# Infini-attention with a gated routed FFN on one core: moving a ReLU and a copy between engines, merging maxima, and timing small products by their reader

## The chip, the cores and the metric

The kernel runs on one core of one Trainium2 chip. A core has five engines that run their own queues in order and meet through semaphores: TensorE (PE in the profile; its weight loads are PEld), VectorE (DVE), ScalarE (ACT), GpSimd (POOL) and SyncE (SP), which here only issues transfers. The time is the device time of the one launch in microseconds; lower is better. A profile shows one execution.

## The reference

The input `A_x` has 2048 tokens of 640 channels. Two branches are mixed token by token, `g * a + (1 - g) * b`, with `g = sigmoid(x . gate_w)`.

Branch `a` is attention with a compressed memory: 32 heads of 20 channels, four segments of 512 tokens.

```python
for s in range(N):                      # N = 4 segments, one after the other
    qs, ks, vs = q[:, :, s], k[:, :, s], v[:, :, s]
    logits = einsum("bhqd,bhkd->bhqk", qs, ks) * scale + mask      # causal, inside the segment
    a_dot = einsum("bhqk,bhkd->bhqd", softmax(logits), vs)
    pq = phi(qs)                        # phi(t) = t + 1 where t > 0, exp(t) elsewhere
    a_mem = einsum("bhld,bhde->bhle", pq, M) / (einsum("bhld,bhd->bhl", pq, z)[..., None] + 1e-6)
    outs.append(g * a_mem + (1.0 - g) * a_dot)                     # g = sigmoid(beta), per head
    pk = phi(ks)
    M = M + einsum("bhld,bhle->bhde", pk, vs);  z = z + einsum("bhld->bhd", pk)
a = concat(outs) @ wo
```

Branch `b` picks the one token with the largest `x . w_r`, runs a SwiGLU FFN with 1728 hidden channels on it alone, and adds the result, weighted by a sigmoid, to that token; all other tokens pass through.

## The kernel before

**Units, jobs, groups.** The 32 heads are two halves of 16. A unit is one half and one segment, so there are eight units, `u` = 0 to 7, the four segments of the first half and then those of the second. A unit has five projection jobs (`projections`, L658): two for q and k over 512 columns, one over 256, two for v over 320 or 322. A job is 15 steps in each of two phases (`pair_up`, L373): every step issues two 64-row matmuls at L392 that run side by side into two PSUM banks. All numbers are split into a high and a low part, and three products (high·high, high·low, low·high) make one product in near full precision. Between the phases stands a drain (the "swap"), because each bank then gets the other half of the rows.

**Projected tiles.** `evac_t` (L460) brings a tile of q or k to SBUF as `phi` (L474 on ScalarE for the even bank, L477 on VectorE for the odd one) and queues "pieces". One splits it into hi (ScalarE, L486) and lo (GpSimd, L490); these go to DRAM and come back stacked as `qs` and `ks`, four places each. Two other pieces make phi(t) = max(t, 0) + exp(min(t, 0)): `neg` = ReLU(−t) on ScalarE (L501), `neg` = exp(−neg) on ScalarE (L507), ReLU of the tile in place on ScalarE (L509), and the sum on GpSimd (L511). `neg` has a single buffer. There are five `phi` places; a projection job waits when they would run out.

**Attention.** A group `n` is four heads of a unit: 32 groups. A group goes through five `a` steps (`a_step`, L724), which compute logits with the query on the partition and take their maximum on VectorE: blocks of 128 queries by up to 512 keys, causal ones through added matmuls with `tri` and `eye`. Steps 0 and 1 hold one block of 512 keys, steps 2 and 3 a block of 384 beside one of 128, step 4 four blocks of 256 at once. L749 issues one reduction per block, L745 one for all of step 4. The maxima are split (GpSimd, L763 and L764), transposed (`m_rows`, L767) and sent into two more rows of `qs`. Then five `b` steps (`b_step`, L789) compute the logits again, with the key on the partition and the maximum subtracted inside the matmul; ScalarE takes the exponential into one of eight `p` places (L800), and GpSimd zeroes what is not causal (L806). `pv_step` (L814) multiplies with v in 32 matmuls of 128×32 shape and ScalarE copies the result to `pvs` (L827), which has one place. `norm` (L841) transposes it, divides by the sum on VectorE (L860 to L865) and adds the memory part on GpSimd (L868).

**Memory.** `keys` (L552) transposes phi(k), `memory_write` (L592) adds to M and z, `memory_read` (L566) computes the memory part of a group. The reads, the writes and PV use the 128×32 shape of the array; projections, logits and transposes use 64×128.

**Output.** When all projections are issued, 16 output tiles follow (`out_stage`, L1092), each after its rows came back from DRAM and were transposed (`out_rows`, L1049: hi on ScalarE at L1066, lo on VectorE at L1068). The FFN runs as a side job between them and the attention.

**What sets the order.** The program is written out by a planner at build time (the loop at L1245). It keeps a modelled time for every engine (`now`), adds an estimate for each operation (`run`, `pe`), and always issues what its model says is ready: transposes of maxima and `turned` work first (transposes of keys, normalisation), then PV, then logits, then one projection step. Four PSUM banks serve projections and small products: two take the sums of the current job, and the other two (`misc`) take PV, reads, writes and transposes. At the next job the pairs swap, so a small product must be read before that.

```python
def misc_ready(n=1, keep=KEEP):                                     # L352
    if filling[0] and not full() and (where[0] == "open" or where[0] == "mid" and left[0] < keep):
        return 1e9
```

`left` is the modelled time still to go in the job, `KEEP` is 1.2 us (1.6 for output tiles). Logits are held back to 2.9 groups behind the projections' progress (`chunks`):

```python
if e and e[1] <= t and e[0] + LEAD <= chunks[0] + ahead and (best is None or e[0] < best[1][0]):   # L1212
```

Memory reads and writes are `chores`; `visit` (L1226) issues those that fit its budget, then PV.

Of the kernel before, what the change touches and what calls it, by code (L numbers as in the profile page):

```python
# [46 lines left out]
LEAD = 2.9  # L47
PR = 8
# [4 lines left out]
KEEP = 1.2  # L53
OKEEP = 1.6
# [11 lines left out]
def tile_infini_mod(  # L66
# [285 lines left out]
    def misc_ready(n=1, keep=KEEP):  # L352

        if filling[0] and not full() and (where[0] == "open" or where[0] == "mid" and left[0] < keep):
            return 1e9
        return sorted(misc_free[i] for i in others())[n - 1]
# [16 lines left out]
    def pair_up(o0, f0, o1, f1, cols, note):  # L373


        n = 3 * KT
        left[0] = 2 * n * us_of(cols)
        for phase in range(2):
            if phase:
                where[0] = "swap"  # L380
                yield 0.0
                nc.tensor.drain()
                pe(0.12)
            use((64, 128))
            where[0] = "mid"
            for i in range(n):
                step_at[0] = max(f(i, r)[2] for f, r in ((f0, phase), (f1, 1 - phase)))
                while step_at[0] > now["PE"]:
                    yield 0.0
                for o, f, r in ((o0, f0, phase), (o1, f1, 1 - phase)):  # L390
                    a, b, ready = f(i, r)
                    nc.tensor.matmul(o, a, b, start=phase == 0 and i == 0, stop=phase == 1 and i == n - 1)  # L392
                note(phase, i)
                left[0] -= us_of(cols)
                yield pe(us_of(cols)) - 0.22
# [60 lines left out]
    phis = {}  # L456

    uses = {}

    def evac_t(u, j, sums, parts):  # L460
# [34 lines left out]
        if s < SEG - 1 or j in QGROUP:  # L495
            state = {}
            uses[u, j] += 1 + (s < SEG - 1) + (s > 0 and j in QGROUP)

            def part():
                r = state["r"] = pool.tile([128, L], F32, tag="neg", bufs=1, name="neg")  # L500
                nc.scalar.activation(r, c, AF.Relu, scale=-1.0)  # L501
                run("ACT", 0.2 + L / 1200, free)

            def rest():
                used()
                r = state["r"]
                nc.scalar.activation(r, r, AF.Exp, scale=-1.0)  # L507
                run("ACT", 0.2 + L / 1200)
                nc.scalar.activation(c, c, AF.Relu)  # L509
                end = run("ACT", 0.2 + L / 1200, split_at[0])  # L510
                nc.gpsimd.tensor_tensor(out=c, in0=c, in1=r, op=OP.add)  # L511
                end = run("POOL", 0.1 + L / 430, end)
                if s < SEG - 1:
                    turned.append((end, lambda: (used(), keys(u, j, c)), lambda: writes[0] == epoch(u)))
# [3 lines left out]
            pieces.extend(((1, part, False), (1, rest, False)))  # L518

# [25 lines left out]
    def first(entries, t, budget=1e9):  # L545

        for e in entries:
            if e[0] <= t and e[-1]() and (len(e) == 3 or e[1] <= budget):
                entries.remove(e)
                return e  # L550

    def keys(u, j, e):  # L552
        keyed[u] = keyed.get(u, 0) + 1
        for r in range(2):
            parts = [t for t in TILES[j] if t[2] == "k" and t[0] // 64 == r]
            if parts:
# [5 lines left out]
                end = pe(0.25)  # L562
                for r0, r1, kind, g, c0 in parts:
                    nc.scalar.copy(kk[:, g, :, c0:c0 + r1 - r0], tp[:, :, r0 - 64 * r:r1 - 64 * r])
                    misc_free[i] = run("ACT", 0.3, end)

    def memory_read(u, g, e):
# [6 lines left out]
        end = pe(0.75, mbd_at[0])  # L574
# [6 lines left out]
        misc_free[i] = run("ACT", 0.55, mid)  # L581
# [9 lines left out]
    def memory_write(u):  # L591
# [9 lines left out]
        end = pe(2.6, va_at[0])  # L601
# [28 lines left out]
    def turn():  # L630
        e = first(turned, now["PE"]) if misc_ready(2) <= now["PE"] else None
        if e:
            e[1]()
            return True
# [89 lines left out]
    def a_step(n, k):  # L724
        use((64, 128))
        if n not in mx:
            mx[n] = pool.tile([128, 2, 2, 4], F32, tag="mx", bufs=3, name="mx")
# [16 lines left out]
        if k == 4:  # L744
            nc.vector.tensor_reduce(out=mx[n][:, :, :, 1], in_=a.rearrange("p b (c t) -> p b c t", c=2), axis=AX.X, op=OP.max)  # L745
            end = run("DVE", 0.16 + 2 / 0.96 * 0.512, end)
        else:
            for i, p, at, w in LOGITS[k]:
                nc.vector.tensor_reduce(out=mx[n][:, :, p, i:i + 1], in_=a[:, :, at:at + w], axis=AX.X, op=OP.max)  # L749
# [9 lines left out]
    def m_split(n):  # L759
        m = mx.pop(n).rearrange("p b c i -> p b (c i)")  # L760
# [6 lines left out]
    def m_rows():  # L767
        if not rows or rows[0][0] > now["PE"] or misc_ready(2) > now["PE"]:
            return False
# [3 lines left out]
        for r in range(2):  # L773
# [5 lines left out]
            misc_free[i] = run("ACT", 0.2, end)  # L779
# [9 lines left out]
    def b_step(n, k):  # L789
# [11 lines left out]
        end = run("ACT", 1.05, end)  # L801
# [12 lines left out]
    def pv_step(n):  # L814
# [12 lines left out]
        nc.scalar.copy(pvs[n], pv)  # L827
        misc_free[i] = run("ACT", 0.6, end)
        turned.append((misc_free[i] + 0.1, lambda: norm(n), lambda: True))
# [11 lines left out]
    def norm(n):  # L841
# [16 lines left out]
        end = pe(0.47)  # L858
# [190 lines left out]
    def out_rows(t):  # L1049
# [12 lines left out]
        done = pe(0.6, ot_at[t])  # L1062
# [21 lines left out]
    def ahead(t):  # L1084
# [3 lines left out]
        if t in ot and not tasks and not loaded and ot_at[t] <= now["PE"] and misc_ready(2, OKEEP) <= now["PE"] + 0.4:  # L1088
            out_rows(t)
            return True  # L1090

    def out_stage():  # L1092
# [3 lines left out]
        for t in range(NT):  # L1096
# [35 lines left out]
            end = misc_free[pair[0]] = run("DVE", 0.5, now["PE"] + 0.22, mixed[t])  # L1132
            half = pool.tile([128, L], F32, tag="neg", bufs=1, name="half")[:, :n]
# [74 lines left out]
    def logits(ahead, t):  # L1208
# [13 lines left out]
    def pv_ready(t):  # L1222
        n = done_pv[0]
        return n < NG and done_b[0] > n and n - 1 not in pvs and p_at[n] <= t and misc_ready() <= t

    def visit(budget, pv):  # L1226
# [6 lines left out]
        for f in side:  # L1233
            if f.last == 2 and side_at[0] <= now["PE"] and misc_ready() <= now["PE"] + 0.2:
                f.step()
# [9 lines left out]
    while True:  # L1245
# [15 lines left out]
        if pv and (where[0] == "open" or blocked or gt > 1e8 or left[0] > 2.0 or over[0] == JOBS * NU):  # L1261
            logits(0.2, t)
            visit(0.7 if where[0] == "mid" else 1.3, True)
            continue
        waits = t - side_at[0] if side and side[0].last == 2 else -1.0
        if where[0] == "swap" and (old or waits >= 0.0) and misc_ready() <= t + 0.2:
            logits(0.2, t)
# [3 lines left out]
        if waits > 3.0 and misc_ready() <= t:  # L1271
            visit(0.7, False)
            continue
        if logits(0.0, t):
# [4 lines left out]
        if logits(1.0 if gt < 1e8 else 99.0, t):  # L1279
# [59 lines left out]
```

## Time and profile before

| | |
|---|---|
| median of 3 runs | 607.3 us (604.44 to 608.02) |
| the profiled execution | 608.08 us, its span 606.4 us |
| TensorE busy | 572.0 us, 94% |
| ScalarE | 383.9 us, 63% |
| VectorE | 338.1 us, 56% |
| GpSimd | 327.0 us, 54% |
| granted TensorE clock | 0.993 |

The span runs from the first to the last instruction of the one profiled execution. Busy time is the union of an engine's instructions, so a busy TensorE can still be slower than it might be. In lists of groups, the number after `x` counts instructions, then come busy us and the mean ns of one, and behind the bar the idle time of that engine just before them with what ended it. A wait "A <- B" is idle time of A's engine that an instruction of B ended; where several things were waited for it names the last.

### The profile page before, as it was taken

The page shows a single profiled execution, that of the slowest core. Times are in us where ns is not written, and L with a number is a line of the kernel's source. Part 1 is how long each engine was busy: PE and PEld are TensorE (multiplying, and loading weights), DVE is VectorE, ACT ScalarE, POOL GpSimd, SP SyncE. Part 2 cuts the span into 40 slices and gives each one's busy share as a digit, 9 for nine tenths or more (in the row PEclk, how much of TensorE's full clock was granted, in tenths as well). Part 3 has the DMA queues.
Part 4 walks back from the last instruction along what each step waited for, and adds up shares of the span by engine and source line. Part 5 has one row for each costly group of instructions (what it writes and reads, how often), then busy time and mean ns, then how long its engine had stood idle before and what let it go on. Part 6 is the DMA issues. An engine that isn't in the chain of part 4 may idle for free.

```text
span 606.4 us, 19959 instructions
## 1 busy us (share of the span) xinstructions
PE 572.0 (94%) x8186; PEld 456.3 (75%) x8186; DVE 338.1 (56%) x614; ACT 383.9 (63%) x681; POOL 327.0 (54%) x443
## 2 busy tenths in 40 slices
PE   6998999999989999999999899999999879989896
PEld 5886976877767877676887667787677667778896
DVE  7433555664565546854556466665465496643432
ACT  8726775876677667766755667675575565555332
POOL 4554656556556966758635634864685343333111
PEclk9999999999989999999999989999999999999999
DMA  7886757536845677678798887576686793424561
GB/s 196 224 277 203 223 149 229 140 126 188 210 135 132 184 211 188 189 213 238 233 274 218 253 245 236 142 239 189 211 239 198 209 262 104 144 82 139 164 197 66
DMA packets 81331, 116.73 MB, mean 193 GB/s; under 512 B 36112, under 2 KB 41752, under 8 KB 81240
## 3 DMA queue, kind: packets, MB, share of 16 engines
q1 hardware_dynamic: 81240, 115.46, 65.1%
q8 instruction: 65, 1.06, 0.8%
q14 instruction: 26, 0.21, 0.1%
HBM read 72.94 MB, written 41.96 MB: 189 GB/s over the span
## 4 chain that ended last, share of the span: by engine, by line
PE 79%; DMA 8%; DVE 5%; ACT 3%; issue 2%; POOL 2%; SPq 1%; POOLq 0%; ACTq 0%; DVEq 0%
PE bank L392 45%; PE bank L821 10%; PE bt L796 7%; PE a L732 6%; DVE mx L749 2%; PE bank L573 2%; PE bank L600 2%; DMA stkk<-hi 2%; PE a L741 2%; DMA raw<-in_xT_dram 2%; SPq L153 1%; PE bank L857 1%; ACT p L800 1%; PE bank L965 1%; DMA ot<-otok 1%
## 5 line engine op out<-in xcount | busy, mean ns | idle before, releaser
L749 DVE TENSOR_REDUCE mx<-a 128x2 f32<-128x768 f32 (+1 forms) x192 | 160.7, 865 | 96.3 <-PE a L741 47.3
L800 ACT ACTIVATE p<-bt 128x1024 f32<-128x1024 f32 x160 | 164.2, 1026 | 60.8 <-PE bt L796 56.3
L806 POOL TENSOR_SCALAR_AFFINE_SELECT p<-p 128x512 f32<-128x512 f32 (+1 forms) x160 | 88.0, 550 | 129.4 <-ACT p L800 103.4
L392 PE MATMUL bank<-xhi,whi 64*128 64x512 f32 (+1 forms) x480 | 101.7, 380 | 2.9 <-issue 0.5
L392 PE MATMUL bank<-xlo,whi 64*128 64x512 f32 (+1 forms) x480 | 101.1, 373 | 0.6 <-POOL xlo L181 0.6
L392 PE MATMUL bank<-xhi,wlo 64*128 64x512 f32 (+1 forms) x480 | 99.4, 368 | 0.0
L732 PE MATMUL a<-ks,qs 60*128 60x384 f32 (+3 forms) x512 | 74.4, 326 | 7.9 <-DVE mx L749 6.3
L796 PE MATMUL bt<-qs,ks 62*128 62x128 f32 (+3 forms) x512 | 75.5, 333 | 4.4 <-ACT p L800 3.7
L821 PE MATMUL bank<-p,va 128*32 128x512 f32 (+3 forms) x1024 | 75.5, 435 | 0.0
L392 PEld LDWEIGHTS bank<-xhi,whi 64*128 64x128 f32 x480 | 56.1, 187 | 14.5 <-issue 11.5
L796 PEld LDWEIGHTS bt<-qs,ks 62*128 62x128 f32 x512 | 49.2, 188 | 18.6 <-issue 7.6
L821 PEld LDWEIGHTS bank<-p,va 128*32 128x32 f32 x1024 | 30.1, 109 | 42.4 <-issue 30.2
L732 PEld LDWEIGHTS a<-ks,qs 60*128 60x128 f32 x512 | 50.2, 187 | 14.6 <-DVE mx L749 8.2
L511 POOL TENSOR_TENSOR phi<-phi,neg 128x512 f32<-128x512 f32 x38 | 49.0, 1288 | 22.4 <-ACT phi L509 20.0
L392 PEld LDWEIGHTS bank<-xlo,whi 64*128 64x128 f32 x480 | 57.5, 188 | 4.0 <-POOL xlo L181 1.6
L490 POOL TENSOR_TENSOR lo<-phi,hi 128x512 fp32r<-128x512 f32 x40 | 51.9, 1298 | 14.7 <-ACT hi L486 7.0
L392 PE MATMUL bank<-whi,xhi 64*128 64x322 f32 (+1 forms) x320 | 58.2, 325 | 1.5
L392 PEld LDWEIGHTS bank<-xhi,wlo 64*128 64x128 f32 x480 | 57.0, 187 | 2.5
L392 PE MATMUL bank<-whi,xlo 64*128 64x322 f32 (+1 forms) x320 | 57.5, 318 | 0.0
L392 PE MATMUL bank<-whi,oh 64*128 64x320 f32 x320 | 51.8, 322 | 6.0 <-DVE ol L1068 4.0
L392 PE MATMUL bank<-wlo,xhi 64*128 64x322 f32 (+1 forms) x320 | 57.3, 319 | 0.0
L827 ACT COPY pvs<-bank 128x512 f32<-128x512 f32 x32 | 18.8, 587 | 56.5 <-PE bank L821 56.4
(119 smaller groups left out, 1088.9 us busy)
## 6 DMA issues: line engine op xcount, KB each, us to landing
qs<-stkq SPq DMA_DIRECT2D x64, 240.0 KB
ks<-stkk SPq DMA_DIRECT2D x64, 240.0 KB
raw<-in_xT_dram SPq DMA_DIRECT2D x40, 256.0 KB
stkq<-hi SPq DMA_DIRECT2D x32, 320.0 KB
stkq<-lo SPq DMA_DIRECT2D x32, 160.0 KB
otok<-ou SPq DMA_DIRECT2D x32, 160.0 KB
xf<-in_x_dram SPq DMA_DIRECT2D x8, 640.0 KB
out_dram<-xf SPq DMA_DIRECT2D x16, 320.0 KB
```

The lines of the kernel that those rows point to most:

```text
L392: nc.tensor.matmul(o, a, b, start=phase == 0 and i == 0, stop=phase == 1 and i == n - 1)
L490: nc.gpsimd.tensor_tensor(out=lo, in0=c, in1=f32(hi), op=OP.subtract)
L511: nc.gpsimd.tensor_tensor(out=c, in0=c, in1=r, op=OP.add)
L573: nc.tensor.matmul(nm[r:r + 32, c, :], e[:GC, 128 * c + r:128 * c + r + 32], mbd[:, g, :], start=True, stop=True)
L600: nc.tensor.matmul(mp[p, g, :], kk[:, g, c, p], va[u % 2][:, c, GW * g:GW * g + GW], start=c == 0, stop=c == 3)
L732: nc.tensor.matmul(a[:, b, at:at + w], q_, ks[n % NS][64 * b:64 * b + ST, p, :w], start=(i, p) == LOGITS[k][0][:2], stop=False)
L749: nc.vector.tensor_reduce(out=mx[n][:, :, p, i:i + 1], in_=a[:, :, at:at + w], axis=AX.X, op=OP.max)
L796: nc.tensor.matmul(bt[:, b, at:at + w], k_, qs[n % NS][64 * b:64 * b + ST + 2, p, L - w:], start=True, stop=True)
L800: nc.scalar.activation(pt, bt, AF.Exp, scale=SCALE)
L806: nc.gpsimd.affine_select(out=d, in_=d, pattern=[[0, e[1]] for e in dims[:-1]] + [[1, 128]], base=0, channel_multiplier=-1, compare_op=OP. ...
L821: nc.tensor.matmul(pv[32 * j:32 * j + 32, 128 * c:], va[u % 2][:, c, VW * h:VW * h + 32], pt_tiles[n, j % 2, c][:, j // 2], start=c == 0, ...
L827: nc.scalar.copy(pvs[n], pv)
```

## The change

- **ReLU.** The ReLU of the tile (L509) becomes a maximum with 0 on GpSimd, ahead of the sum on the same engine.
- **PV copy.** L827 moves from ScalarE to VectorE.
- **Maxima.** Every `a` step has one reduction over 2 × 512 columns. Steps 2 and 3 write four maxima each, and after step 3 a small reduction puts the three of the longer block together. `mx` is larger and has two buffers instead of three.
- **Small products.** `misc_ready` gets a kind. From a table it takes the time that the product's reader needs and the engine of that reader, and admits the product while the time left in the job covers 0.34 us, that time, and the engine's backlog.
- **Places.** Nine places for exponentials instead of eight (at the start they also hold loads).
- **Pacing.** `LEAD` goes; logits are issued whenever their buffers and inputs are ready. `visit` gets 1.7 or 2.5 us instead of 0.7 or 1.3. Normalisation waits in the plan until the group's memory read has been issued.
- **Prices.** Several estimates of the planner change.
- **Output tile.** Pending phi pieces that still use `neg` are issued before the tile takes that buffer for `half`.

```diff
-LEAD = 2.9
-PR = 8
+PR = 9
-KEEP = 1.2
-OKEEP = 1.6
+SLACK = 0.1
+OSLACK = 0.1
...
-    def misc_ready(n=1, keep=KEEP):
+    AFTER = {"rows": (0.4, "ACT"), "keys": (0.6, "ACT"), "norm": (1.26, "DVE"), "read": (0.8, "ACT"), "write": (0.5, "DVE"),
+             "pv": (0.7, "DVE"), "ffn": (0.6, "DVE"), "out": (1.4, "DVE")}
+    def misc_ready(n=1, kind="read", slack=SLACK):
+        us, engine = AFTER[kind]
+        if filling[0] and not full() and (where[0] == "open" or where[0] == "mid" and left[0] + slack < 0.34 + us + max(
+                now[engine] - now["PE"] - 0.3, 0.0)):
             return 1e9
...
                 nc.tensor.drain()
-                pe(0.12)
+                pe(0.3)
...
             def rest():
                 used()
+                unread.pop(0)
                 r = state["r"]
                 nc.scalar.activation(r, r, AF.Exp, scale=-1.0)
                 run("ACT", 0.2 + L / 1200)
-                nc.scalar.activation(c, c, AF.Relu)
-                end = run("ACT", 0.2 + L / 1200, split_at[0])
+                nc.gpsimd.tensor_scalar(c, c, 0.0, None, op0=OP.max)
+                end = run("POOL", 0.9, split_at[0])
                 nc.gpsimd.tensor_tensor(out=c, in0=c, in1=r, op=OP.add)
...
-            if e[0] <= t and e[-1]() and (len(e) == 3 or e[1] <= budget):
+            if e[0] <= t and e[-1]() and (misc_ready(2, e[1]) <= t if e[1] in AFTER else e[1] <= budget):
...
-            mx[n] = pool.tile([128, 2, 2, 4], F32, tag="mx", bufs=3, name="mx")
+            mx[n] = pool.tile([128, 2, 2, 16], F32, tag="mx", bufs=2, name="mx")
...
-            nc.vector.tensor_reduce(out=mx[n][:, :, :, 1], in_=a.rearrange("p b (c t) -> p b c t", c=2), axis=AX.X, op=OP.max)
-            end = run("DVE", 0.16 + 2 / 0.96 * 0.512, end)
+            o, parts = mx[n][:, :, :, 4], 2
+        elif k < 2:
+            o, parts = mx[n][:, :, k, 12:13], 1
         else:
-            for i, p, at, w in LOGITS[k]:
-                nc.vector.tensor_reduce(out=mx[n][:, :, p, i:i + 1], in_=a[:, :, at:at + w], axis=AX.X, op=OP.max)
-                end = run("DVE", 0.16 + w / 480, end)
+            o, parts = mx[n][:, :, k - 2, :4], 4
+        nc.vector.tensor_reduce(out=o, in_=a.rearrange("p b (c t) -> p b c t", c=parts), axis=AX.X, op=OP.max)
+        end = run("DVE", 0.16 + 2 / 0.96 * 0.512, end)
         free["a"] = end + 0.1
         done_a[0] += 1
+        if k == 3:
+            nc.vector.tensor_reduce(out=mx[n][:, :, :, 8], in_=mx[n][:, :, :, 1:4], axis=AX.X, op=OP.max)
+            run("DVE", 0.16)
...
-        nc.scalar.copy(pvs[n], pv)
-        misc_free[i] = run("ACT", 0.6, end)
-        turned.append((misc_free[i] + 0.1, lambda: norm(n), lambda: True))
+        nc.vector.tensor_copy(pvs[n], pv)
+        misc_free[i] = run("DVE", 0.69, end)
+        turned.append((misc_free[i] + 0.1, "norm", lambda: norm(n), lambda: u % SEG == 0 or n in om))
...
+            while unread:
+                e = unread[0]
+                while e in pieces:
+                    pieces.pop(0)[1]()
             half = pool.tile([128, L], F32, tag="neg", bufs=1, name="half")[:, :n]
...
-            if e and e[1] <= t and e[0] + LEAD <= chunks[0] + ahead and (best is None or e[0] < best[1][0]):
+            if e and e[1] <= t and (best is None or e[0] < best[1][0]):
...
-            visit(0.7 if where[0] == "mid" else 1.3, True)
+            visit(1.7 if where[0] == "mid" else 2.5, True)
```

The estimates that change: the drain as above, transposes of keys 0.25 to 0.14, a memory read 0.75 to 0.6 and its copy 0.55 to 0.45, a write 2.6 to 2.3, the exponential 1.05 to 1.03, the copy of the transposed maxima 0.2 to 0.16, the transposes of a normalisation 0.47 to 0.25 and of an output tile 0.6 to 0.5.

More of the change, by code (lines that the diff above doesn't have):

```diff
@@ L767, in m_rows @@
     def m_rows():
-        if not rows or rows[0][0] > now["PE"] or misc_ready(2) > now["PE"]:
+        if not rows or rows[0][0] > now["PE"] or misc_ready(2, "rows") > now["PE"]:
             return False
@@ L1087, in ahead @@
         fetch_rows(t + 1)
-        if t in ot and not tasks and not loaded and ot_at[t] <= now["PE"] and misc_ready(2, OKEEP) <= now["PE"] + 0.4:
+        if t in ot and not tasks and not loaded and ot_at[t] <= now["PE"] and misc_ready(2, "out", OSLACK) <= now["PE"] + 0.4:
             out_rows(t)
@@ L1233, in visit @@
         for f in side:
-            if f.last == 2 and side_at[0] <= now["PE"] and misc_ready() <= now["PE"] + 0.2:
+            if f.last == 2 and side_at[0] <= now["PE"] and misc_ready(1, "ffn") <= now["PE"] + 0.2:
                 f.step()
@@ L1270, in tile_infini_mod @@
             continue
-        if waits > 3.0 and misc_ready() <= t:
+        if waits > 3.0 and misc_ready(1, "ffn") <= t:
             visit(0.7, False)
             continue
-        if logits(0.0, t):
+        if logits(t):
             continue
```

38 lines of the change are left out of this document (19 added, 19 removed).

## The prediction

> **What bounds the kernel now.** I read the totals and the chain on the page first, then the waits of TensorE, then the timeline around the longest of them, then the groups by shape for the prices. The page:
>
> ```profile
> span 606.4 us, 19959 instructions
> ...
> PE 572.0 (94%) x8186; PEld 456.3 (75%) x8186; DVE 338.1 (56%) x614; ACT 383.9 (63%) x681; POOL 327.0 (54%) x443
> ...
> PE 79%; DMA 8%; DVE 5%; ACT 3%; issue 2%; POOL 2%; SPq 1%; POOLq 0%; ACTq 0%; DVEq 0%
> ```
>
> TensorE is busy for 572.0 of 606.4 us and holds 79% of the chain; the next engine, ScalarE, is busy 63%. So a microsecond taken off ScalarE, VectorE or GpSimd is worth nothing by itself. It is worth something where TensorE stands still for that engine, or where the plan sends TensorE a better order of work. The idle time of TensorE is 606.4 − 572.0 = 34.4 us. The waits view says who ended it (engine, line, tile, releaser: total us, times, longest):
>
> ```profile
> PE a L732 <- DVE mx L749: 6.3, 7, 2.6
> PE bank L138 <- DVE identf L131: 4.2, 1, 4.2
> PE bank L392 <- DVE ol L1068: 4.0, 4, 1.6
> PE bt L796 <- ACT p L800: 3.7, 7, 1.6
> PE bank L776 <- ACT kk L564: 1.6, 1, 1.6
> PE a L732 <- DVE rs L860: 0.7, 1, 0.7
> ```
>
> The 4.2 us on identf are the start of the program, and the tail after the last projection is as fixed. The longest waits are traced one by one in the timeline (start us, length us, engine, line, operation, idle before it):
>
> ```profile
> 484.61 0.83 DVE L1014 TENSOR_TENSOR kk<-kk,y 128x640 f32<-128x640 f32 x1 [4.13 <-DMA y<-yrow]
> 487.21 0.50 PE L732 MATMUL a<-ks,qs 60*128 60x512 f32 x2 [2.62 <-DVE mx L749]
> ...
> 345.79 0.62 ACT L178 CAST xhi<-raw 128x512 fp32r<-128x512 f32 x1 [2.85 <-DMA raw<-in_xT_dram]
> 347.38 0.50 PE L796 MATMUL bt<-qs,ks 62*128 62x384 f32 x4 [1.59 <-ACT p L800]
> ...
> 54.53 0.63 ACT L501 ACTIVATE neg<-phi 128x512 f32<-128x512 f32 x1 [1.38 <-POOL phi L511]
> ```
>
> The 2.6 us wait for a maximum is really a transfer: VectorE stood 4.13 us at L1014 for the FFN row, and the maximum was queued behind it. The 1.6 us wait for an exponential is a transfer too: ScalarE stood 2.85 us for a load of x. Neither is touched by any edit. The third is of the kind that the change reaches: ScalarE stood 1.38 us for GpSimd's phi because `neg` has one buffer, and kk (1.6 us of TensorE) came late behind it. What is left within the change's reach is 6.3 − 2.6 = 3.7 for maxima, 3.7 − 1.6 = 2.1 for exponentials, 1.6 for kk and 0.7 for rs: **8.1 us**. The 4.0 us on ol belong to the output tiles, whose transposes keep nearly the same gate (a remainder of 1.6 us before; 0.34 + 1.4 − 0.1 = 1.64 us after).
>
> **The change part by part.** The prices, from groups by shape (busy us, mean ns, then idle before):
>
> ```profile
> L749 DVE TENSOR_REDUCE mx<-a 128x2 f32<-128x1024 f32 x64 | 78.3, 1223 | 48.8 <-PE a L739 45.3 <-POOL phi L511 1.9 <-PE bank L776 1.0
> L749 DVE TENSOR_REDUCE mx<-a 128x2 f32<-128x768 f32 x64 | 61.2, 956 | 47.4 <-PE a L741 47.3
> L745 DVE TENSOR_REDUCE mx<-a 128x4 f32<-128x1024 f32 x32 | 39.2, 1226 | 27.1 <-PE a L741 25.7 <-PE bank L392 1.2
> L749 DVE TENSOR_REDUCE mx<-a 128x2 f32<-128x256 f32 x64 | 26.6, 416 | 0.0
> L477 DVE COPY phi<-bank 128x512 f32<-128x512 f32 x16 | 10.9, 682 | 3.2 <-PE bank L392 3.2
> L892 DVE TENSOR_REDUCE best<-rg 128x1 f32<-128x16 f32 x1 | 0.2, 170 | 0.1
> ...
> L509 ACT ACTIVATE phi<-phi 128x512 f32<-128x512 f32 x38 | 23.8, 625 | 8.6 <-POOL lo L490 8.6
> L827 ACT COPY pvs<-bank 128x512 f32<-128x512 f32 x32 | 18.8, 587 | 56.5 <-PE bank L821 56.4
> ...
> L806 POOL TENSOR_SCALAR_AFFINE_SELECT p<-p 128x512 f32<-128x512 f32 x96 | 61.9, 645 | 70.0 <-ACT p L800 49.5 <-ACT mr L778 15.1 <-DMA qs<-mr 2.0
> L511 POOL TENSOR_TENSOR phi<-phi,neg 128x512 f32<-128x512 f32 x38 | 49.0, 1288 | 22.4 <-ACT phi L509 20.0 <-ACT mr L778 2.3
> ```
>
> *Maxima.* Steps 2 and 3 of a group are now two reductions, 956 + 416 = 1372 ns; as one over 1024 elements they cost what L745 costs, 1226 ns. That is 146 ns in 64 steps, 9.3 us of VectorE. Added are 32 small reductions, which I price at the 170 ns of L892: 5.4 us. They are queued behind the maximum of step 3, after buffer `a` is free, and VectorE then waits for TensorE's next step anyway (25.7 us in L745's row), so that wait hides them; without it they would cost their 5.4 us. On TensorE only the waits for a maximum get shorter: 7 waits by 0.146 us would be 1.0 at most; not all are behind such steps, so I take −0.7. `mx` with two buffers instead of three costs nothing: a group's maxima are split long before the group after next begins.
>
> *PV copy.* ScalarE loses 32 × 587 ns = 18.8 us and the head-of-queue wait for PV of 56.4 us; VectorE gains both, with 32 × 682 ns (L477, the same shape from PSUM) = 21.8 us. This is the one place where a wait moves to another queue: behind the copy on VectorE stand the next maxima, the four products and the reciprocal of the normalisation, and the odd bank's evacuations. TensorE's next `a` step waits for the first, the next projection job for the last. The bank of PV itself comes free 95 ns later, 32 × 0.095 = 3.0 us at most. The copy comes behind the maximum that is issued before PV, and maxima of later steps can't start until TensorE has left PV, so the delay on a maximum is about the copy less the next step's own matmuls. Bounds: 0 where a projection pair fills TensorE (it usually does: 94% busy), 32 × 0.682 = 21.8 us where none does. I take +1.0, near the lower end, because the same wait on ScalarE in front of exponentials costs TensorE only 3.7 us in all now.
>
> *ReLU.* ScalarE loses 23.8 us and the 8.6 us wait on GpSimd's lo; together with the copy, ScalarE falls from 383.9 to 341 us. GpSimd gets 38 operations with one tensor in and one out. Before shows none of this form; the nearest is the select of the same shape, 645 ns, the far end is the two-input add, 1288 ns: 24.5 to 48.9 us, taken as 24.5 because it too has one input. GpSimd goes to 352 (376 at the far end) of 606 us, still idle for 40%. What is queued behind it is the add on the same tile, then selects that PV waits for. The order was exp, ReLU on ScalarE, then the add; now the ReLU runs beside exp, so the add can begin some 0.6 us sooner and `neg` comes free sooner. It can lose as much where GpSimd is behind. Inside the waits below.
>
> [...]
>
> *Pacing.* `LEAD` kept logits from running closer than 2.9 groups behind the projections. Does it bind? Two windows, from the start to the end of the fifth unit (the first row the projections' line, the second the exponentials):
>
> ```profile
> 0.00:278.30 278.30, 169.45 (x1500) 124.39 (x1502) 0.99 0.68 191
> ...
> 0.00:278.30 278.30, 77.02 (x75) 0.99 0.68 191
> ```
>
> A unit has 300 projection matmuls, so 1500 are five units, 20 groups; 75 exponentials are 15 groups. The lag is 5 groups, above 2.9, so there the logits wait for PV, buffers and transfers and not for `LEAD`. Taken at 0; if it matters in the first units, it moves work forward and not away. The ninth place for exponentials lets one more `b` step go ahead of a late PV: of the 2.1 us I take −0.8 (0 to −2.1). At the start a ninth raw load finds room too, worth 0.
>
> *Order.* A budget per visit of 1.7 or 2.5 us instead of 0.7 or 1.3 lets memory reads, which the plan prices at 0.8 us, join PV: none or one before, two or three now. Both use the 128×32 shape of the array, and a change of shape shows up:
>
> ```profile
> 212.66 0.16 PEld L821 LDWEIGHTS bank<-p,va 128*32 128x32 f32 x8 [0.24 <-issue]
> ...
> 214.95 0.30 PEld L796 LDWEIGHTS bt<-qs,ks 62*128 62x128 f32 x4 [0.20 <-issue]
> ...
> L573 PE MATMUL bank<-mbd,phi 80*32 80x84 f32 x768 | 17.6, 240 | 0.0
> ```
>
> 0.24 us going in and 0.20 us coming out make 0.44 us for each visit saved. There are 768 / 32 = 24 reads. Between 0 and 24 × 0.44 = 10.6 us, I take ten reads, −4.4. [...] Timing the small products by their reader (time that reader needs, plus its backlog) in place of one remainder of 1.2 us admits the short ones later in a job and keeps them out when the reader is behind. The new prices stand closer to the rows (0.69 for a copy of 682 ns). I let that and the shorter ScalarE queue remove half of the 8.1 us: −4.0 (bounds: +8, as many new waits again, to −8.1). The normalisation now waits until its memory read is done, which could hold the single `pvs` place and so the next PV; nothing of that shows before, priced at 0, at the far end half a microsecond for 24 groups, 12 us. No DMA is added; their order on SP's queue follows the plan.
>
> **The sum.** −0.7 + 1.0 − 0.8 − 4.4 − 4.0 = −8.9 us, against the profiled execution's own 608.1 us (span 606.4): **599**. That execution is 0.8 us above the median of 607.3. One per cent, about what a measurement of this kernel can tell from no change, puts the bounds at 601.2 and 613.4.
>
> **The rivals.**
> 1. *No net change, 607.* All moved work was hidden, and a new order makes as many new waits as it takes away. For it: the two longest waits are late transfers that the plan mispriced, and nothing here prices transfers better. Against it: the shape changes saved don't depend on luck. Gives 603 to 611.
> 2. *Slower: VectorE is held by the PV copy, 619.* The place is the copy at the head of VectorE's queue, with maxima behind it. Its price is 0.682 us for each of 32 groups, at most 21.8 us; at half of them 608 + 11 = 619. It decides from the point where TensorE's waits for maxima, now 6.3 us, pass about 15. For it: those are already the largest wait. Against: VectorE is idle 44%.
> 3. *Logits unpaced and more work let in, well faster, 588.* Every wait within reach goes (−8.1) and the reads nearly all join PV (−10.6): 608.1 − 18.7 = 589, with the ninth place 588.
> 4. *GpSimd late, 615.* The ReLU takes the 1288 ns of the two-input add, 38 × 0.64 = 24.4 us more than I took. If a quarter of that reaches PV through the selects, 6 us, and the gain on waits and reads doesn't come, the time is 608 + 6, about 615. [...] Against it:
>
> ```profile
> POOL p L806 <- ACT p L800: 103.4, 76, 5.2
> ```
>
> GpSimd stood 103.4 us waiting for exponentials ahead of the selects, so most of it has cover.
>
> **How the numbers follow.** The forecast has 0.50, rival 1 0.18, rival 2 0.12, rival 3 0.15, rival 4 0.05. The forecast's own range is 592 to 604; about 0.08 of all lies in it above 601.2. Faster: 0.42 of the forecast + 0.15 of rival 3 = 0.57. Slower: 0.12 of rival 2 + 0.04 of rival 4 = 0.16. Within 1%: the rest, 0.08 + 0.18 + 0.01 = 0.27. The range is 584 to 613: it leaves out most of rivals 2 and 4 (0.14) and a little below rival 3 (0.05), where the bounds of the reads and the waits are both reached and a wait that I called a transfer's goes too.
>
> **What would show it.** In the page after: ScalarE near 341, VectorE near 338.1 − 9.3 + 5.4 + 21.8 = 356, GpSimd near 352 us; TensorE still above 94%. One L749-like group of 1226 ns in all steps. The PV copy with some 56 us of waits on VectorE. TensorE's waits for maxima and exponentials under 7 us together; if those for maxima grow past 15, rival 2 is right. Fewer stays in the 128×32 shape, with two or more reads beside a PV. The prediction is wrong if TensorE's idle time other than the 4.2 us of start isn't smaller, or if its busy time rises because the reads moved apart from PV.

## The result, and the profile after

The changed kernel takes 612.5 us (median of 15 runs) against 608.25 us in runs beside it: ratio **1.0077, interval 1.0051 to 1.0103**. It is slower by 0.8%. I had forecast 599 us and a faster kernel; the time lies inside the range, but the sign is wrong. By the bounds that the prediction set itself (601.2 to 613.4) it counts as no change, which had a chance of 0.27.

The page of the changed kernel, totals and chain, as read for the kernel before:

```profile
span 613.0 us, 19941 instructions
...
PE 574.3 (94%) x8186; PEld 459.9 (75%) x8186; DVE 357.3 (58%) x613; ACT 349.3 (57%) x611; POOL 384.6 (63%) x482
...
PE 69%; POOL 8%; ACT 6%; DMA 6%; issue 5%; DVE 4%; SPq 1%; POOLq 0%; ACTq 0%; DVEq 0%
```

TensorE has the same work (8186 matmuls) and is as busy. Its idle time rose from 34.4 to 613.0 − 574.3 = 38.7 us, which the prediction named as a sign that it is wrong. GpSimd went from 327.0 to 384.6 us, now the second busiest engine, and from 2% to 8% of the chain. The groups that the change moved (busy us, mean ns, idle before and what ended it):

```profile
L514 POOL TENSOR_SCALAR phi<-phi 128x512 f32<-128x512 f32 x38 | 56.8, 1493 | 3.3 <-ACT neg L505 2.2
L505 ACT ACTIVATE neg<-phi 128x512 f32<-128x512 f32 x38 | 24.0, 631 | 36.3 <-POOL phi L516 36.3
L838 DVE COPY pvs<-bank 128x512 f32<-128x512 f32 x32 | 22.1, 692 | 58.7 <-PE bank L832 55.6 <-ACT xhi L177 1.7 <-ACT neg L512 1.4
L756 DVE TENSOR_REDUCE mx<-a 128x8 f32<-128x1024 f32 x64 | 78.2, 1222 | 39.1 <-PE a L747 37.8 <-PE bank L787 0.7
```

The copy and the maxima cost what was forecast. The ReLU doesn't: **1493 ns** on GpSimd, above both ends of my bounds (645 and 1288 ns) and above the 0.9 us that the plan counts. And ScalarE stands 36.3 us in front of `neg`, waiting for GpSimd's sum to give the one buffer back; it was 9.8 us before (total us, times, longest):

```profile
ACT neg L501 <- POOL phi L511: 9.8, 10, 1.6
```

The waits of TensorE in the changed kernel, without those of the start and of the output tiles, which changed little:

```profile
PE bt L807 <- ACT p L811: 8.1, 6, 4.7
...
PE bank L567 <- ACT phi L478: 2.4, 1, 2.4
PE bank L579 <- ACT va L627: 2.1, 1, 2.1
PE bank L567 <- POOL phi L514: 1.8, 1, 1.8
PE bank L567 <- DVE ou L876: 1.4, 1, 1.4
PE a L738 <- DVE mx L756: 1.2, 2, 0.6
```

Waits for maxima nearly vanished (6.3 to 1.2 us), waits for exponentials doubled (3.7 to 8.1), and waits for transposes and evacuations are new. The longest is 4.7 us. The timeline of the changed kernel there (start, length, engine, line, idle before):

```profile
373.26 1.11 POOL L989 TENSOR_TENSOR fe<-fe,fg 128x432 f32<-128x432 f32 x1 [5.20 <-DVE fe L987]
...
376.79 1.48 POOL L514 TENSOR_SCALAR phi<-phi 128x512 f32<-128x512 f32 x1
378.35 1.26 POOL L516 TENSOR_TENSOR phi<-phi,neg 128x512 f32<-128x512 f32 x1
...
379.64 0.63 ACT L505 ACTIVATE neg<-phi 128x512 f32<-128x512 f32 x1 [6.95 <-POOL phi L516]
...
381.90 0.80 PE L807 MATMUL bt<-qs,ks 62*128 62x384 f32 x4 [4.70 <-ACT p L811]
```

ReLU and sum take GpSimd from 376.79 to 379.61. ScalarE waits 6.95 us for that buffer with the next exponential queued behind, and TensorE stands 4.70 us for the exponential. GpSimd was late to begin with: two products of the FFN stood ahead of these in its queue, and it had waited 5.20 us for VectorE before the first (L989). The 1.48 us of the ReLU are only a part of this stop: in the same order with the ReLU on VectorE (a run below) it is still 3.29 us.

Some stops have a stretch at half clock behind them, and may cost more than their own length by it. Stretches of 3.4 us in the changed kernel (start and end, length, busy time with count of PE, PEld, DVE, ACT and POOL, the granted clock, DMA share, GB/s):

```profile
29.90:33.30 3.40, 3.40 (x36) 3.40 (x34) 0.41 (x1) 0.67 (x2) 2.60 (x3) 0.50 0.91 295
60.60:64.00 3.40, 3.40 (x19) 3.14 (x16) 1.23 (x1) 1.53 (x4) 3.32 (x5) 0.50 0.87 303
381.40:384.80 3.40, 2.90 (x16) 2.43 (x18) 0.00 (x0) 1.48 (x2) 3.26 (x4) 0.51 0.26 70
480.40:483.80 3.40, 3.40 (x24) 1.49 (x20) 0.43 (x2) 0.44 (x1) 0.73 (x1) 0.50 0.82 221
500.90:504.30 3.40, 3.40 (x26) 3.32 (x26) 3.23 (x5) 2.81 (x5) 1.82 (x2) 0.50 0.93 231
```

and in the kernel before:

```profile
171.60:175.00 3.40, 3.00 (x25) 2.50 (x27) 2.23 (x4) 2.28 (x5) 0.85 (x2) 0.50 0.05 11
349.10:352.50 3.40, 3.40 (x34) 2.39 (x34) 1.75 (x4) 1.39 (x2) 1.20 (x2) 0.50 0.86 270
```

TensorE's granted clock there is 0.50 or 0.51. Apart from the tail there are five such stretches now and two before: 10.2 us more at half speed, up to 5.1 us lost (an estimate, half of the 10.2), beside 4.3 us more idle. Together that is more than the 6.6 us by which the span grew, so by this reckoning the rest of TensorE's work got a little shorter, and the stops took more than that back. These are two single executions, though, and their clocks differ more than usual: 0.984 against 0.993, where the 15 runs of the changed kernel average 0.988 and the kernel before 0.990 in the batches below. A clock lower by 0.002 over some 610 us is about 1.2 us, an estimate, of the 4.2 us between the medians.

### The profile page after: what moved, and what is told of

Same layout as the page of the kernel before. It is cut to its first block, busy times and chain, and to the rows that moved or that the text cites. A ratio compares the mean times of both kernels' runs of the same rounds, so it can differ in the third digit from the quotient of the medians.

```text
span 613.0 us, 19941 instructions
## 1 busy us (share of the span) xinstructions
PE 574.3 (94%) x8186; PEld 459.9 (75%) x8186; DVE 357.3 (58%) x613; ACT 349.3 (57%) x611; POOL 384.6 (63%) x482
## 3 DMA queue, kind: packets, MB, share of 16 engines
q8 instruction: 64, 1.05, 0.7%
## 4 chain that ended last, share of the span: by engine, by line
PE 69%; POOL 8%; ACT 6%; DMA 6%; issue 5%; DVE 4%; SPq 1%; POOLq 0%; ACTq 0%; DVEq 0%
PE bank L397 38%; PE bank L832 9%; PE bt L807 6%; PE a L738 5%; POOL phi L514 3%; PE bank L579 2%; POOL phi L516 2%; DMA raw<-in_wc_dram 2%; PE a L747 2%; DMA raw<-in_xT_dram 2%; ACT p L811 1%; SPq L152 1%; PE bank L606 1%; PE bank L976 1%; ACT neg L505 1%
## 5 line engine op out<-in xcount | busy, mean ns | idle before, releaser
L756 DVE TENSOR_REDUCE mx<-a 128x2 f32<-128x1024 f32 (+2 forms) x160 | 195.7, 1223 | 94.0 <-PE a L747 49.3
L811 ACT ACTIVATE p<-bt 128x1024 f32<-128x1024 f32 x160 | 164.1, 1026 | 99.9 <-PE bt L807 96.2
L397 PE MATMUL bank<-xlo,whi 64*128 64x512 f32 (+1 forms) x480 | 99.0, 372 | 0.3 <-POOL xlo L180 0.3
L807 PE MATMUL bt<-qs,ks 62*128 62x384 f32 (+3 forms) x512 | 74.3, 331 | 8.1 <-ACT p L811 8.1
L832 PE MATMUL bank<-p,va 128*32 128x512 f32 (+3 forms) x1024 | 77.3, 442 | 0.2 <-ACT num L586 0.2
L738 PE MATMUL a<-ks,qs 60*128 60x384 f32 (+3 forms) x512 | 71.8, 320 | 1.2 <-DVE mx L756 1.2
L807 PEld LDWEIGHTS bt<-qs,ks 62*128 62x128 f32 x512 | 48.5, 187 | 20.8 <-ACT p L811 10.2
L832 PEld LDWEIGHTS bank<-p,va 128*32 128x32 f32 x1024 | 32.5, 111 | 40.7 <-issue 30.4
L397 PE MATMUL bank<-wlo,xhi 64*128 64x322 f32 (+1 forms) x320 | 59.2, 324 | 0.0
L397 PE MATMUL bank<-whi,xlo 64*128 64x322 f32 (+1 forms) x320 | 59.1, 320 | 0.0
L514 POOL TENSOR_SCALAR phi<-phi 128x512 f32<-128x512 f32 x38 | 56.8, 1493 | 3.3 <-ACT neg L505 2.2
L838 DVE COPY pvs<-bank 128x512 f32<-128x512 f32 x32 | 22.1, 692 | 58.7 <-PE bank L832 55.6
```

The costliest lines, as they stand in the source:

```text
L514: nc.gpsimd.tensor_scalar(c, c, 0.0, None, op0=OP.max)
L738: nc.tensor.matmul(a[:, b, at:at + w], q_, ks[n % NS][64 * b:64 * b + ST, p, :w], start=(i, p) == LOGITS[k][0][:2], stop=False)
L756: nc.vector.tensor_reduce(out=o, in_=a.rearrange("p b (c t) -> p b c t", c=parts), axis=AX.X, op=OP.max)
L807: nc.tensor.matmul(bt[:, b, at:at + w], k_, qs[n % NS][64 * b:64 * b + ST + 2, p, L - w:], start=True, stop=True)
L811: nc.scalar.activation(pt, bt, AF.Exp, scale=SCALE)
L832: nc.tensor.matmul(pv[32 * j:32 * j + 32, 128 * c:], va[u % 2][:, c, VW * h:VW * h + 32], pt_tiles[n, j % 2, c][:, j // 2], start=c == 0, ...
```

## The experiments

The planner makes causes hard to part: whatever changes a price changes the order of everything behind it. So eleven of the eighteen runs keep an order to the last instruction and change only which engine does an operation, how many reductions there are, or a buffer; the planner still counts the work where it was. Ratios, with a 95% interval, are to the kernel before in the same batch; they needn't be the quotient of the medians.

### The ReLU, replanned

**Back on ScalarE**, the rest as changed:

```diff
-                nc.gpsimd.tensor_scalar(c, c, 0.0, None, op0=OP.max)
-                end = run("POOL", 0.9, split_at[0])
+                nc.scalar.activation(c, c, AF.Relu)
+                end = run("ACT", 0.2 + L / 1200, split_at[0])
```

> The changed kernel with the ReLU of phi back on ScalarE (625 ns), all else as changed. Theory 1, the ReLU on GpSimd costs the time (1493 ns each where 645 was assumed, ScalarE then stands for the one neg buffer, 36.3 us against 9.8): 598 to 604 us, ScalarE's wait for the sum on GpSimd back near 10 us. Theory 2, the new order (no pacing, larger budgets, gate by reader) costs it: stays 610 to 615. Theory 3, the PV copy at the head of VectorE's queue: stays 610 to 615.

608.8 us, ratio 1.0006 (0.9984 to 1.0029). ScalarE's wait for the sum is down to 3.0 us. The loss is gone, but no gain comes: not the 598 to 604 that I expected. The order is another one too, so this run alone doesn't show that the ReLU was the loss.

**Only its price corrected**, 0.9 to 1.5 us:

> The changed kernel with only the planner's price of the ReLU on GpSimd raised from 0.9 to 1.5 us; the same work in another order. Theory 1 in its form 'the plan is misled by 0.6 us each': 602 to 607. If it is GpSimd's time itself and the single neg buffer, which the plan does not count at all: 610 to 615, ScalarE's wait for the sum still above 25 us.

632.4 us, ratio 1.0372 (1.0325 to 1.0419). Both readings of the time fail, though ScalarE's wait for the sum, 31.4 us, is above 25 as the second had it. The plan is nearer the truth and the kernel is 20 us worse.

**On VectorE**, priced 0.42 us:

> The changed kernel with the ReLU on VectorE (same operation, priced 0.42 us in the plan). Theory 1: 597 to 604, GpSimd near 330 us busy, ScalarE's wait for the sum near 10 us. Theories 2 and 3: 610 to 615, and by theory 3 rather more, since VectorE gets more work.

630.4 us, ratio 1.0349 (1.0303 to 1.0394), and ScalarE's wait for the sum is 28.3 us, not near 10. Against theory 1, until the next runs showed that the order did it.

**Only the order rules, prices and the ninth place**, all three moves of work undone:

> The changed kernel with the ReLU and the PV copy back on ScalarE and the maxima one per block again: only the order rules, the prices and the ninth place of the change are left. Theory 1: no slower than before, 600 to 608. Theory 2: 611 to 616 although no engine's work has changed. Theory 3: 600 to 608.

613.3 us, ratio 1.0085 (1.0055 to 1.0116): slower than before with every operation on its old engine. Theory 2 can't be dropped after these four.

### One operation at a time, order fixed

**Old order, ReLU on GpSimd:**

```diff
-                nc.scalar.activation(c, c, AF.Relu)
+                nc.gpsimd.tensor_scalar(c, c, 0.0, None, op0=OP.max)
                 end = run("ACT", 0.2 + L / 1200, split_at[0])
```

> The kernel before, its instruction order kept to the last one (the planner still counts the ReLU as ScalarE's), with only the ReLU of phi done on GpSimd. Theory 1, the move of the ReLU costs time by itself (1493 ns on GpSimd, so neg comes free later and ScalarE stands for it): 610 to 620, ScalarE's wait for the sum on GpSimd from 9.8 to above 25 us. Theory 2, only the order matters and the engines have slack: 606 to 610.

615.7 us, ratio **1.0118** (1.0087 to 1.0149). Its group in this run, and ScalarE's wait for the sum (total us, times, longest):

```profile
L509 POOL TENSOR_SCALAR phi<-phi 128x512 f32<-128x512 f32 x38 | 56.8, 1494 | 2.5 <-ACT neg L501 1.8
```

```profile
ACT neg L501 <- POOL phi L511: 24.1, 11, 3.7
```

The same 1494 ns in another order; ScalarE's wait goes from 9.8 to 24.1 us. The move costs time by itself. The trace shows a part of the path: the wait for kk that the prediction traced to the single `neg` buffer (1.6 us of TensorE at 54 us) is now 2.9 us, behind a ScalarE that stood 2.29 us for GpSimd's phi, and the longest wait for a maximum grew from 2.6 to 3.7 us. Neither stop was followed by half clock in the kernel before; now each is, for 6.8 us. In all TensorE was idle for 3.8 us more and at half clock for 10.2 us more, up to 5.1 us lost, and this execution's span was 9.1 us longer.

**Old order, PV copy on VectorE** (`nc.vector.tensor_copy` at L827):

> The kernel before, in its own order, with only the copy of the PV result on VectorE. If a copy at the head of VectorE's queue holds maxima (my rival 2): 612 to 620 and TensorE's waits for maxima above 10 us. If it is hidden or helps ScalarE: 603 to 609.

608.8 us, ratio 1.0016 (0.9985 to 1.0047). TensorE's waits for maxima were 5.2 us in its profile; rival 2 isn't what happened in this order.

**Old order, merged maxima:**

> The kernel before, in its own order, with only the maxima merged (one reduction per step and a small one after step 3). My term was -0.7 us: 606 to 609. If the small reduction or the wider merged one holds buffer a: 610 or more.

609.05 us, ratio 1.0011 (0.9983 to 1.0039): nothing, and −0.7 us couldn't be told from nothing.

**New order, ReLU and PV copy done on ScalarE:**

> The changed kernel in its own order, with the ReLU and the PV copy done on ScalarE as before (the planner still counts them as GpSimd's and VectorE's). Theory 1: 600 to 608, since the 1493 ns operations are gone. Theory 2, the order itself is the worse one: 611 to 620, as ScalarE now has 42 us more than the plan knows of.

633.1 us, ratio 1.0412 (1.0381 to 1.0443). The new order is laid out for a ScalarE without these 42 us: TensorE's waits for exponentials rise to 22.8 us. It tells that an order is tied to the durations it was planned with, and it doesn't judge the ReLU.

**New order, ReLU on VectorE**, still counted as GpSimd's:

```diff
-                nc.gpsimd.tensor_scalar(c, c, 0.0, None, op0=OP.max)
+                nc.vector.tensor_scalar(c, c, 0.0, None, op0=OP.max)
                 end = run("POOL", 0.9, split_at[0])
```

> The changed kernel in its own order, with only the ReLU done on VectorE instead of GpSimd (the planner still counts it as GpSimd's). Replanned with its price on VectorE, the same work took 630 us. Theory 1, the GpSimd operation is what costs: 600 to 606 here, below the kernel before, and the 630 came from the other order. If a ReLU on VectorE is bad in itself: 615 to 630 again.

608.0 us, ratio 0.9993 (0.9969 to 1.0017), against 1.0077 with GpSimd: the whole loss is won back. It isn't below the kernel before, which I had expected it to be. From its groups, and from its waits:

```profile
L514 DVE TENSOR_SCALAR phi<-phi 128x512 f32<-128x512 f32 x38 | 18.8, 495 | 14.9 <-POOL lo L494 10.5 <-ACT neg L505 3.3 <-ACT hi L490 1.1
```

```profile
ACT neg L505 <- POOL phi L516: 21.3, 12, 5.5
```

495 ns instead of 1493, and a wait of 21.3 instead of 36.3 us. Against the changed kernel's profile, TensorE's idle time fell from 38.7 to 33.6 us and its time at half clock, without the tail, from 17.1 to 10.2 us. The 630 us of the replanned version was the order's.

**Old order, ReLU and sum as one VectorE operation** (`scalar_tensor_tensor`, maximum then add):

> The kernel before in its own order, with the ReLU and the sum of phi made by one VectorE operation, max(c, 0) + neg, in place of ScalarE's 625 ns and GpSimd's 1288 ns. If the waits for the single neg buffer (9.8 us on ScalarE) and the length of the phi chain matter: 600 to 606. If that chain has slack in the old order: 606 to 610.

613.5 us, ratio 1.0082 (1.005 to 1.0113), although it takes 43 us off GpSimd. The 812 ns operation stands in front of maxima: TensorE's waits for them at the first reduction line went from 6.3 to 10.8 us.

### How much an order is worth

Two nudges of a price, with no operation changed: the ReLU at 1.0 us instead of 0.9 in the changed kernel, and the exponential at 1.03 us instead of 1.05 in the kernel before (its mean there is 1026 ns).

> The changed kernel with the planner's price of the ReLU on GpSimd at 1.0 us instead of 0.9: nothing but the order changes. If the time of an order is a matter of luck of some per cent (a price of 1.5 gave 632), this lies anywhere from 605 to 630; if a price nearer to the 1493 ns makes it steadily worse, 613 to 620; if the order is robust, 611 to 614.

622.8 us, ratio 1.0215 (1.0176 to 1.0254).

> The kernel before with the planner's price of an exponential at 1.03 us instead of 1.05 (measured: 1026 ns), which is one of the price edits of the change: nothing but the order changes. If orders scatter by luck: anywhere from 600 to 625. If the kernel before is robust to such a nudge: 606 to 610.

615.95 us, ratio 1.0143 (1.0101 to 1.0186). Each is 1.4% above the kernel that it was nudged from (1.0215 / 1.0077 and 1.0143), though nothing about the work changed. These two medians are of four runs each. In the second, the waits view of TensorE shows how little it takes:

```profile
PE bank L1061 <- DMA ot<-otok: 5.1, 1, 5.1
```

The order had put the transposes of an output tile ahead of a transfer that came 5.1 us later, and 6.8 us at half clock followed. Much of what an order costs shows up that way. Without the tail, this execution ran at half clock for 20.5 us, the nudged changed kernel's for 30.7 and that with the ReLU priced at 1.5 us for 51.2, of which 20.5 us in one piece from 137 us on behind a stop of 4.8 us; the kernel before had 6.8. If half of such time is lost, an upper estimate, then of the 24.4 us by which the span with the price of 1.5 us exceeds that of before, up to 22 come this way.

**Budgets alone** in the kernel before (1.7 and 2.5 us):

> The kernel before with only the budgets of a visit raised to 1.7 and 2.5 us, so that memory reads may join PV. My term for it was -4.4 us: 601 to 606 and ten stays fewer in the 128x32 shape. If the reads don't join, or the new order's luck outweighs it: 606 to 620.

610.0 us, ratio 1.0012 (0.9986 to 1.0038). Counted in the traces (memory writes and FFN products included), the stays in the 128×32 shape fell from 57 to 52, and 13 of them hold a read beside PV (3 before); in the whole change they fell to 54, and 10 hold a read beside PV. So the reads did join PV. Five stays fewer are 2.2 us by my price; new waits of 2.0 and 2.2 us for transfers of `qs` and `ks`, and 6.8 us more at half clock, may have taken that back, which isn't shown.

### The single buffer of neg

**Two buffers for `neg`** in the kernel before, old order, nothing else:

```diff
-                r = state["r"] = pool.tile([128, L], F32, tag="neg", bufs=1, name="neg")
+                r = state["r"] = pool.tile([128, L], F32, tag="neg", bufs=2, name="neg")
```

> The kernel before in its own order with two buffers for neg and nothing else, as the base of the run above. It takes away 9.8 us of ScalarE's waits, one of which is in front of TensorE's 1.6 us wait at 54 us: 604 to 608. If ScalarE only waits elsewhere then: 607 to 610.

605.6 us, ratio **0.995** (0.9925 to 0.9975): faster than both kernels. TensorE's 1.6 us wait for kk at 54 us is gone.

**The same with the ReLU on GpSimd:**

> The kernel before in its own order, with the ReLU on GpSimd and two buffers for neg instead of one. With one buffer this took 615.7 us (+1.2%). If the single buffer is how the slow ReLU reaches TensorE (ScalarE standing 24.1 us at L501): 606 to 610 and that wait under 8 us. If it is GpSimd's time itself, which delays the phi tiles and the selects: 612 to 616 although the wait is gone.

610.1 us, ratio 1.0035 (1.0005 to 1.0064), where one buffer gave 1.0118. The wait in this run's trace:

```profile
ACT neg L501 <- POOL phi L511: 3.2, 2, 2.5
```

24.1 us became 3.2, and TensorE's stop for kk, 2.9 us with one buffer, is gone. So the buffer is part of the path. Measured against its own base, the slow ReLU still costs 1.0035 / 0.995 = 1.0085, so GpSimd's time itself, by paths other than the buffer, is most of the cost. How much the buffer adds isn't settled: 1.2% against 0.85% is a difference of 0.3%, and by the intervals it could be nothing.

### Can VectorE take it all?

**Old order, ReLU and PV copy on VectorE and merged maxima:**

> The kernel before in its own order, with all three moves of work at once, but the ReLU on VectorE: ReLU and PV copy on VectorE, merged maxima. PV copy and maxima alone were +0.2% and +0.1%, both within their intervals; a ReLU of 495 ns on VectorE in place of 625 on ScalarE should free neg sooner: 604 to 609. If VectorE's queue gets too long for the maxima, as with the fused operation (+0.8%): 611 to 616.

616.1 us, ratio 1.0116 (1.0077 to 1.0154).

**Old order, only the ReLU on VectorE:**

> The kernel before in its own order with only the ReLU on VectorE. All three moves together took 616.1 us there (+1.2%). If the ReLU in VectorE's queue, which waits for GpSimd's lo, holds the maxima behind it: 611 to 616. If it is the three together that are too much for VectorE: 606 to 610.

615.1 us, ratio 1.0136 (1.0091 to 1.0181; the quotient of the medians is 1.0095): it does it alone. TensorE's waits for maxima in this run:

```profile
PE a L732 <- DVE mx L749: 10.4, 11, 2.5
...
PE a L732 <- DVE mx L745: 1.6, 2, 1.0
```

12.0 us, 6.9 before. The ReLU waits in VectorE's queue for GpSimd's lo (9.6 us) with maxima behind it. In the old order ScalarE is the best of the three places for this operation; in the new order VectorE beat GpSimd, and the ReLU alone on ScalarE in that order wasn't tried.

**Two buffers and merged maxima**, old order:

> The kernel before in its own order with two buffers for neg and the merged maxima. Two buffers alone took 605.6 us (ratio 0.995), merged maxima alone +0.1% within their interval. If the two add: 603 to 608. If the merged maxima delay buffer a once ScalarE is quicker: 608 to 611.

606.9 us, ratio 0.9966 (0.9936 to 0.9995): below the kernel before, and not better than two buffers alone.

## Why the prediction was wrong, point by point

1. **The ReLU is the step that failed.** "Taken as 24.5 because it too has one input", with nothing in the sum for what it does to TensorE: it took 56.8 us, and the move cost 0.8 to 1.2%. The far end, the two-input add, wasn't an upper bound either: the add took 1285 ns and the ReLU 1493, so here another operation of the same shape on the same engine bounded nothing. The row of the add said how GpSimd does one instruction, not how it does this one, and a split by the number of inputs, read from the select and the add, doesn't hold for it. This step turned no change into a loss; that the gain of 8.9 us didn't come either is points 4 and 5.
2. **"The add can begin some 0.6 us sooner and `neg` comes free sooner."** With 645 ns it would have. With 1493 the ReLU outlasts ScalarE's exponential by 0.86 us: the add, which stood behind 633 + 625 ns on ScalarE, now stands behind at least 1493, and behind whatever else GpSimd has queued, so `neg` comes free later. I had the right resource in front of me, in the third stop quoted from the timeline, and put the wrong sign on it. Three comparisons with the order held fixed give the cost of this move: +1.2% in the old order, +0.85% there with two buffers, and −0.8% when VectorE takes it off GpSimd in the new order. The replanned ones say less, since the order moves with them: −0.7% on ScalarE, but +2.7% on VectorE.
3. **Rival 4 was the nearest**, GpSimd late, at 615 us with a chance of 0.05. Its price was too small, and its cover was misread: the 103.4 us that GpSimd waited for exponentials lie in other places than the ReLU, whose row has 3.3 us of idle time in front of it. Idle time of an engine isn't cover unless it falls where the operation is queued. GpSimd took 1493 ns for this one-input maximum, VectorE 495 ns for the same 512 columns in the new order.
4. **The −4.4 us for reads that join PV.** The reads joined, about as many as forecast: 11 of the 24 stand beside a PV in the change, 3 before. But the stays fell by 3, 1.3 us by my price instead of 4.4. The step that failed is that each read beside a PV saves a stay. Before, 21 reads without PV shared 14 stays; in the change the 13 that are left still take 12. With the budgets alone the stays fell by 5 and the time stayed. The price of 0.44 us for a stay was an estimate from two gaps, 0.24 and 0.20 us. No run shows that a change of shape makes them or that they cost TensorE as much: behind the first of them in the same timeline, with no change of shape, PV's own weight loads at 213.11, 213.54 and 213.87 us have 0.30, 0.30 and 0.19 us idle before them.
5. **The −4.0 us for waits that a better plan removes.** This had no mechanism behind it. TensorE's idle time rose. A replanned order moved the time by 1.4%, 9 us, at the smallest nudges of a price, so a term of 4 us for "better prices" was below what any such edit can be trusted for, and its sign was a guess. That the range of 584 to 613 held the time was luck in part: with the ReLU priced at 1.5 us, the correct price, the same work came out at 632.
6. **Right:** the maxima (no change to be seen with them alone in the old order, VectorE at 357.3 us against a forecast of 356), the PV copy (692 ns, 55.6 us of waits moved to VectorE, no cost to be seen alone in the old order), and pacing: without `LEAD` the planner writes the same program for the kernel before. ScalarE fell to 349, not 341.
7. **Missing altogether:** the half-clock stretches behind stops, though two, besides the one at the end, were in the trace of before.

What stays open: the rest of the change comes out at no difference with the ReLU on VectorE in the same order, or replanned on ScalarE. What a ReLU on VectorE costs in that order isn't known, so the rest may be a little better than it looks. The order rules with the old engines were 0.8% slower, but an order's scatter is as large, so that the rules themselves are bad isn't shown. The ninth place wasn't tried alone. By which path GpSimd's own time, beyond the buffer, reaches TensorE wasn't pinned down; nor was why one stop is followed by half clock and another isn't.

## What to carry to other kernels

Price an operation that the trace doesn't show as unknown, above the dearest neighbour too, until one run has measured it: here one unmeasured instruction of 1.5 us turned a change that is neutral with that operation on VectorE into a loss. Where a planner writes the order, test a move of work with the order held fixed, and never credit a new order with a few microseconds; nudge a price first to see how far orders scatter. A wait that an engine spends on a single buffer with other work queued behind it, as ScalarE's 6.95 us at 373 us, is a cheap place to look: a second buffer gained 0.5%, where the whole change lost 0.8%.

## What the hardware did that I had not expected

TensorE's granted clock drops to 0.50, for 3.4 us at a time in the two kernels and for 6.8 and 20.5 us in other runs, in most cases shortly behind a stop. In the changed kernel the five stretches quoted above follow stops of 2.4 us (at 26 us), 1.8 (at 58), 4.7 (at 377), 0.8 (at 478) and three short ones of 1.4 us in all (at 497). Stops of 1.7 us at 77 and 2.1 us at 405 brought none, so a stop's length alone doesn't decide. The five stretches begin 30.7, 320.8, 99.0 and 20.5 us apart, which are 9, 94, 29 and 6 times 3.41 us, the length of each in the trace's clock record. The stops in front of four of the five are shorter than that, 0.8 to 2.4 us. What sets off a stretch isn't shown.

In the changed kernel a one-input maximum with a constant took GpSimd 1493 ns for 512 columns, longer than adding two tensors (1285 ns), while a causal select of the same shape took 650 ns.
